# Block-causal attention and a gated FFN in one kernel: softmax's division moved behind P times V, its reciprocals transposed onto the feature partitions, sums kept per group, lag to the transposes 10 -> 6

## The chip, the cores and the metric

The kernel runs on one core of a Trainium2 chip. Its metric is the device time of one execution in microseconds (us); lower is better. Three runs of the kernel before the change took 1388.63, 1390.05 and 1391.88 us, so the median is 1390.05 us.

A core has TensorE (PE in the profile, with its weight loads in a row of their own, PEld), VectorE (DVE), ScalarE (ACT), GpSimd (POOL) and SyncE (SP), which here only issues DMAs. Each engine takes its instructions in the order in which they were built. Matrix products land in PSUM, which has eight banks here, each of 512 fp32 columns on 128 partitions.

## The reference, cut to what matters

```python
batch, n_heads, seq, head_dim = (8, 8, 576, 64)
scores = matmul(q, k.transpose(0, 1, 3, 2)) / sqrt(64)
scores = where(pos[:, None] // 64 >= pos[None, :] // 64, scores, -1e9)
scores = scores - max(scores, axis=-1, keepdims=True)
attn = exp(scores)
attn = attn / (sum(attn, axis=-1, keepdims=True) + 1e-09)
x = matmul(attn, v).transpose(0, 2, 1, 3).reshape(4608, 512)
h = x @ w_in                                    # 512 -> 2048
P = a[0] + a[1] * h + a[2] * h**2 + a[3] * h**3
Q = 1.0 + abs(b[0]) * abs(h) + abs(b[1]) * h**2
out = (P / (Q + 1e-6)) @ w_out                  # 2048 -> 512
```

All inputs and the output are fp32. Every large product is taken as three products of values that are split into a high and a low part.

## The kernel before, in words

**Attention** goes by pairs of heads: 8 batches of 4 pairs make 32 *visits*. A visit has five query tiles t = 0 to 4 (64 queries, then four times 128, lists `NQ` and `Q0`) with 64 to 576 keys (`NK`), and two heads j; each (t, j) is a *step*, so a visit has ten steps and the program 320. The names of tiles carry the visit first: s24_1_0_0 is a score tile of visit 24, query tile 1, head 0.

For a step, `scores` (L403) multiplies queries by keys into a PSUM bank (L421, L422, and L425 for the mask), and VectorE takes the negated row maximum (L426). One step later `expo` (L432) has ScalarE write exp into p and add each row's sum into sm (L438). After the second head of a tile, GpSimd adds 1e-9 to the sums (L445), VectorE takes the reciprocals (L446), and GpSimd multiplies them into p: the first 64 keys of both heads go into pk (L447), the other keys stay in place (L451). `transp` (L455) transposes pk and p by TensorE through PSUM (L470; for t = 0 the source has 64 partitions), ScalarE copies out the high part (L475) and VectorE the low part (L476), into pt0, pt1 and pt2. `pv` (L479) multiplies V by them (L489), for group g = 0 (t = 0, 1, 2, 320 queries) and g = 1 (t = 3, 4, 256 queries). The result has the features of both heads on the 128 partitions and queries along the row. ScalarE and VectorE split it into the tile x (L492, L493; tag "xs", one buffer), and a DMA on SyncE's queue stores it in the scratch tensor xscr (L494).

`prep` (L344) makes the next visit's transposed q and k (tp, L355) and the tiles kq by DMA. `vprep` (L374) splits V (L382, L383).

**The FFN** takes 18 chunks of 256 tokens in two phases, 10 of the 16 hidden blocks in phase 0 and 6 in phase 1. A *unit* is a chunk and two hidden blocks: `first` (L190) is 24 products into h (L201) and the first elementwise work, `recip` (L216) and `split` (L228) the rest of it, `second` (L238) 12 products (L250). A chunk can be loaded (L185) when the batches that hold its tokens are in xscr. Phase 0 is woven into the attention; what is left of it and phase 1 run after it.

**The order.** `attn_steps` (L502) emits scores at step k, `expo` at k + 1, and for j = 1 `transp` at k + min(ALAG3, nxt[k] - 1); nxt is the distance to the same tile of the next visit, 10, so ALAG3 = 10 gives a lag of 9. `pv` comes one step behind the transposes of t = 2 and t = 4. The loop at L565 emits FFN units by step: from E0 = 40 + ALAG3 + 3 on (53), up to the chunks that are ready. The Tile layer then orders each engine's instructions with a timeline of its own, so an instruction may stand elsewhere in its engine's queue than it was emitted, and a tile waits until its buffer's last reader is done. Scores, transposes, products and FFN share PSUM: five banks in ps_a, one in ps_h, two in ps_o.

## Time and profile before

| what | value |
|---|---|
| median of three runs | 1390.05 us |
| the profiled execution, its own time | 1389.48 us |
| its span, first to last instruction | 1387.7 us |
| PE busy in the span | 1294.4 us (93%) |
| PE weight loads busy | 1165.6 us (84%) |
| DVE, ACT, POOL busy | 1029.0, 909.7, 955.3 us (74, 66, 69%) |
| first FFN product (L201) | about 134 us |
| last store of an attention result (L494) issued | 982.1 us |

So the span has three stretches: attention and the splitting of the weights alone (0 to 134 us), attention woven with FFN phase 0 (134 to 985 us), and the FFN alone (985 us to the end). In a row of a view by groups stand line, engine, operation, tile written and tiles read, shape, count, then busy us in total, mean ns of one, and idle time of the engine ahead of it with what ended it. In a row of the stretches stand the engines' busy time in that stretch, the instructions in brackets, the granted TensorE clock, the share of the DMA engines and GB/s. A busy PE is not PE at its peak, since products are pipelined: of two that follow each other the second starts before the first ends.

### The profile page before, as it was taken

To read this page: it belongs to the slowest core of one execution; us is meant where nothing else is said; L and a number is where in the kernel's file an instruction comes from. 1 tells how busy PE (TensorE), PEld (TensorE's weight loads), DVE (VectorE), ACT (ScalarE), POOL (GpSimd) and SP (SyncE) were. 2 spreads that over 40 slices of the span, in tenths; PEclk is the share of its full clock that TensorE was granted. 3 is DMA by queue.
4 is the path that set the end of the run, shared out by engine and by line. 5 is a ranking of instruction groups with operands and counts; after the bars stand their busy time and mean duration, and the time that the engine had idled before them with its cause. 6 is when DMAs were issued, how large, how long until landed. Compare 5 with 4: busy or idle time off the path is not lost.

```text
span 1387.7 us, 25820 instructions
## 1 busy us (share of the span) xinstructions
PE 1294.4 (93%) x8736; PEld 1165.6 (84%) x8736; DVE 1029.0 (74%) x2048; ACT 909.7 (66%) x2250; POOL 955.3 (69%) x1240
## 2 busy tenths in 40 slices
PE   4677899999899989999999999999989999999998
PEld 3567788989788878888989999999979998999897
DVE  5898877788778867887767777766756676776665
ACT  4676777777677766776767777776545555555553
POOL 4888877687777757777767676766556655565564
PEclk9787899999999999999999999999999999999999
DMA  9778566666656665675654565651711333333332
GB/s 214 199 196 234 146 148 161 158 165 184 149 142 154 162 167 141 156 178 136 164 133 113 150 151 123 152 139 46 259 59 60 107 122 122 122 122 122 122 122 91
DMA packets 225635, 200.93 MB, mean 145 GB/s; under 512 B 132064, under 2 KB 195552, under 8 KB 225504
## 3 DMA queue, kind: packets, MB, share of 16 engines
q1 hardware_dynamic: 225440, 199.28, 54.2%
q8 instruction: 70, 1.15, 0.3%
q14 instruction: 61, 0.50, 0.1%
q0 software_dynamic: 64, 0.00, 0.0%
HBM read 98.57 MB, written 44.04 MB: 103 GB/s over the span
## 4 chain that ended last, share of the span: by engine, by line
PE 72%; DVE 9%; DMA 6%; POOL 5%; ACT 4%; issue 2%; SPq 1%; DVEq 0%; POOLq 0%; ACTq 0%
PE h L201 26%; PE o L250 25%; PE o L489 9%; PE t L470 4%; PE s L421 3%; PE s L422 3%; PE tp L355 2%; DMA x<-xscr 2%; DMA kq<-hl 2%; DVE nm L426 1%; ACT p L438 1%; POOL gl L234 1%; DVE v L225 1%; DVE u L224 1%; DMA xscr<-x 1%
## 5 line engine op out<-in xcount | busy, mean ns | idle before, releaser
L201 PE MATMUL h<-x,wih 128*128 128x256 f32 x2304 | 446.3, 289 | 12.0 <-DMA x<-xscr 7.9
L201 PEld LDWEIGHTS h<-x,wih 128*128 128x128 f32 x2304 | 372.3, 194 | 21.6 <-issue 7.6
L201 PE MATMUL h<-x,wil 128*128 128x256 f32 x1152 | 331.0, 287 | 0.0
L250 PE MATMUL o<-woh,gl 128*128 128x512 f32 x576 | 232.2, 403 | 7.9 <-POOL gl L234 6.8
L210 POOL TENSOR_SCALAR v<-u,bab 128x512 f32<-128x512 f32 x144 | 120.2, 835 | 165.0 <-ACT u L208 162.6
L250 PE MATMUL o<-woh,gh 128*128 128x512 f32 x576 | 227.9, 396 | 0.0
L250 PE MATMUL o<-wol,gh 128*128 128x512 f32 x576 | 227.0, 394 | 0.0
L426 DVE TENSOR_REDUCE nm<-s 128x1 f32<-128x288 f32 (+4 forms) x384 | 161.4, 427 | 84.8 <-PE s L425 49.9
L201 PEld LDWEIGHTS h<-x,wil 128*128 128x128 f32 x1152 | 223.2, 194 | 0.4
L234 POOL TENSOR_TENSOR gl<-s,gh 128x512 fp32r<-128x512 f32 x144 | 188.4, 1309 | 50.2 <-ACT gh L233 47.2
L438 ACT ACTIVATE p<-s,nm 128x288 f32<-128x288 f32 (+4 forms) x384 | 184.6, 484 | 47.1 <-DVE nm L426 34.8
L211 POOL TENSOR_TENSOR u<-v,u 128x512 f32<-128x512 f32 x144 | 190.2, 1321 | 9.8
L451 POOL TENSOR_SCALAR p<-p,rc 128x128 f32<-128x128 f32 (+3 forms) x256 | 165.0, 656 | 31.6 <-DVE rc L446 29.3
L208 ACT ACTIVATE u<-h 128x512 f32<-128x512 f32 x144 | 86.0, 597 | 123.5 <-PE h L201 116.9
L218 ACT ACTIVATE v<-u,qcb 128x512 f32<-128x512 f32 x144 | 104.6, 726 | 92.0 <-POOL u L211 91.4
L421 PE MATMUL s<-kq 128*128 128x256 f32 (+3 forms) x384 | 136.3, 357 | 24.0 <-DMA kq<-hl 11.2
L212 DVE TENSOR_TENSOR s<-s,h 128x512 f32<-128x512 f32 x144 | 98.6, 685 | 69.8 <-ACT s L209 68.9
L250 PEld LDWEIGHTS o<-woh,gl 128*128 128x128 f32 x576 | 109.4, 190 | 28.3 <-POOL gl L234 9.0
L250 PEld LDWEIGHTS o<-wol,gh 128*128 128x128 f32 x576 | 108.7, 189 | 22.4
L250 PEld LDWEIGHTS o<-woh,gh 128*128 128x128 f32 x576 | 109.3, 190 | 16.0
L470 PE MATMUL t<-ident,p 128*128 128x128 f32 (+1 forms) x672 | 113.0, 279 | 7.2 <-POOL p L451 2.3
L422 PE MATMUL s<-kq 128*128 128x256 f32 (+3 forms) x384 | 119.0, 312 | 0.0
(105 smaller groups left out, 2993.6 us busy)
## 6 DMA issues: line engine op xcount, KB each, us to landing
kq<-hl SPq DMA_DIRECT2D x64, 432.0 KB, 4.2
x<-xscr SPq DMA_DIRECT2D x96, 256.0 KB, 3.6
kq<-hl SPq DMA_DIRECT2D x64, 288.0 KB, 5.4
xscr<-x SPq DMA_DIRECT2D x32, 320.0 KB, 4.7
qr<-in_q_dram SPq DMA_DIRECT2D x64, 144.0 KB, 2.8
kr<-in_k_dram SPq DMA_DIRECT2D x64, 144.0 KB, 2.7
kq<-hl SPq DMA_DIRECT2D x64, 144.0 KB, 4.9
pscr<-os SPq DMA_DIRECT2D x18, 512.0 KB, 3.3
```

The lines of the kernel that those rows point to most:

```text
L201: nc.tensor.matmul(h[:, j, :], lhsT=w[:, dc, fs], rhs=xs[dc // 2][:, dc % 2, hl, :], start=(dc == 0 and i == 0), stop=(dc == 3 and i == 2))
L210: nc.gpsimd.tensor_scalar(out=vt, in0=ut, scalar1=b1, scalar2=b0, op0=ALU.mult, op1=ALU.add)
L211: nc.gpsimd.tensor_tensor(out=ut, in0=vt, in1=ut, op=ALU.mult)
L234: nc.gpsimd.tensor_tensor(out=gl.rearrange("p j t -> p (j t)"), in0=st, in1=gh.rearrange("p j t -> p (j t)").bitcast(F32), op=ALU.subtract)
L250: nc.tensor.matmul(self.o[m], lhsT=g[:, j, ms], rhs=w[:, f, :], start=(u == 0 and j == 0 and i == 0), stop=(u == nu - 1 and j == 1 and i = ...
L421: nc.tensor.matmul(ps[:, :ww], lhsT=kq[:, 0, qs], rhs=kq[:, 1, c0:c0 + ww], start=True, stop=False)
L422: nc.tensor.matmul(ps[:, :ww], lhsT=kq[:, 0, qs], rhs=kq[:, 2, c0:c0 + ww], start=False, stop=not last)
L426: nc.vector.reduce_max(out=nm[:nq, j, i:i + 1], in_=ps[:nq, :w], axis=AX.X, negate=True)
L438: nc.scalar.activation(out=pt[:nq, j, c0:c0 + w], in_=banks[i][:nq, :w], func=AF.Exp, bias=nm[:nq, j, 0:1], scale=1.0, accum_out=sm[:nq, j ...
L451: nc.gpsimd.tensor_scalar(out=pt[:nq, jj, 64:n], in0=pt[:nq, jj, 64:n], scalar1=rc[:nq, jj:jj + 1], scalar2=1.0, op0=ALU.mult, op1=ALU.mult)
L470: nc.tensor.transpose(ps[:, i, :nq], src, ident[:nq, :nq])
L489: nc.tensor.matmul(o[:, s0:w], lhsT=vblock(vv, x), rhs=pp, start=(x == 0 and i == 0), stop=(x == nb - 1 and i == 2))
```

## The change

`expo` no longer divides. The row sums go straight into two tiles that stay for the whole program, sums[0] for t = 0, 1, 2 and sums[1] for t = 3, 4 (with a third column for the second piece of t = 4). GpSimd only copies the first 64 keys into pk (now L447, a copy, and none for t = 0). After t = 2 and after t = 4 one addition of 1e-9 (L455) and one reciprocal (L456) serve the whole group. The tile of t = 0 becomes p0 with 128 partitions whose lower half stays zero, and all transposes take 128 partitions (L474).

A new function `scale` stands right behind the transposes of t = 2 and t = 4: for each query tile of the group GpSimd spreads the reciprocals of both heads over 2 x 64 columns (rb, L491, one buffer), TensorE transposes that into a bank r (L492), and ScalarE copies the bank into the second half of the tile x (L495). In `pv` VectorE multiplies the product by it (L511), ScalarE takes the high part (L512), and GpSimd, no longer VectorE, takes the low part (L513). The store to xscr therefore waits for GpSimd. ALAG3 goes from 10 to 6: the transposes stand 6 steps behind instead of 9, E0 becomes 49, and the other bounds that hold ALAG3 move with it.

```diff
--- before.py
+++ after.py
@@ -31,7 +31,7 @@
 KQB = 3
 XB = 3
 HOLD = 6
-ALAG3 = 10
+ALAG3 = 6
 OFFS = {5:(0,3,5)}
 G1 = 0
 W0 = 36
@@ -305,6 +305,11 @@
         pt1 = [apers.tile([128, 4, 256], F32R, name=f"pt1{x}") for x in "hl"]
         pt2 = [apers.tile([128, 9, 256], F32R, name=f"pt2{x}") for x in "hl"]
 
+        p0 = apers.tile([128, 2, 64], F32, name="p0")
+        nc.vector.memset(p0[64:128], 0.0)
+        sums = [apers.tile([128, 3, 2], F32, name=f"sum{g}") for g in range(2)]
+        nc.vector.memset(sums[0], 1.0)
+
         vpad = [apers.tile([128, 128 + 4 * 192], F32R, name=f"vp{x}") for x in "hl"]
         for x in pt1:
             nc.vector.memset(x[:, 2:4, 0:128].bitcast(F32), 0.0)
@@ -404,13 +409,12 @@
             s = st_[p]
             nq = NQ[t]
             if j == 0:
-                pt = att.tile([128, 2, NK[t]], F32, name=f"p{p}_{t}", tag=f"p{t}", bufs=1)
+                pt = att.tile([128, 2, NK[t]], F32, name=f"p{p}_{t}", tag=f"p{t}", bufs=1) if t > 0 else p0
+                nm = att.tile([128, 2, 2], F32, name=f"nm{p}_{t}", tag="nm", bufs=4)
 
                 pk = att.tile([128, 2, 64], F32, name=f"pk{p}_{t}", tag="pk", bufs=2) if t > 0 else pt
-                nm = att.tile([128, 2, 2], F32, name=f"nm{p}_{t}", tag="nm", bufs=4)
-                sm = att.tile([128, 2, 2], F32, name=f"sm{p}_{t}", tag="sm", bufs=4)
-                s[t] = (pt, pk, nm, sm)
-            pt, pk, nm, sm = s[t]
+                s[t] = (pt, pk, nm)
+            pt, pk, nm = s[t]
             kq = s["kq", j]
             qs = slice(Q0[t], Q0[t] + 128)
             banks = []
@@ -432,28 +436,28 @@
         def expo(p, t, j):
             s = st_[p]
             nq, n = NQ[t], NK[t]
-            pt, pk, nm, sm = s[t]
+            pt, pk, nm = s[t]
+            g, i0 = ((0, t), (1, t - 3))[t > 2]
             banks = s.pop((t, j))
             for i, (c0, w) in enumerate(pieces(t)):
                 nc.scalar.activation(out=pt[:nq, j, c0:c0 + w], in_=banks[i][:nq, :w], func=AF.Exp,
-                                     bias=nm[:nq, j, 0:1], scale=1.0, accum_out=sm[:nq, j, i:i + 1])
-            if j == 0:
+                                     bias=nm[:nq, j, 0:1], scale=1.0,
+                                     accum_out=sums[g][:nq, i0 + i, j:j + 1])
+            if j == 1 and t > 0:
+                nc.gpsimd.tensor_copy(out=pk, in_=pt[:, :, 0:64])
+            if j == 0 or t not in (2, 4):
                 return
-            rc = att.tile([128, 2], F32, name=f"rc{p}_{t}", tag="rc", bufs=4)
-            if t == 4:
-                nc.gpsimd.tensor_tensor(out=sm[:, :, 0], in0=sm[:, :, 0], in1=sm[:, :, 1], op=ALU.add)
-            nc.gpsimd.tensor_scalar_add(rc[:nq], sm[:nq, :, 0], 1e-9)
-            nc.vector.reciprocal(rc[:nq], rc[:nq])
-            nc.gpsimd.tensor_tensor(out=pk[:nq], in0=pt[:nq, :, 0:64],
-                                    in1=rc[:nq].unsqueeze(2).to_broadcast([nq, 2, 64]), op=ALU.mult)
-            if t > 0:
-                for jj in range(2):
-                    nc.gpsimd.tensor_scalar(out=pt[:nq, jj, 64:n], in0=pt[:nq, jj, 64:n],
-                                            scalar1=rc[:nq, jj:jj + 1], scalar2=1.0,
-                                            op0=ALU.mult, op1=ALU.mult)
+
+            nt = (3, 2)[g]
+            rc = att.tile([128, 3, 2], F32, name=f"rc{p}_{g}", tag="rc", bufs=2)
+            if g:
+                nc.gpsimd.tensor_tensor(out=sums[1][:, 1], in0=sums[1][:, 1], in1=sums[1][:, 2], op=ALU.add)
+            nc.gpsimd.tensor_scalar_add(rc[:, :nt], sums[g][:, :nt], 1e-9)
+            nc.vector.reciprocal(rc[:, :nt], rc[:, :nt])
+            s["rc", g] = rc
 
         def transp(p, t):
-            pt, pk, _, _ = st_[p].pop(t)
+            pt, pk, _ = st_[p].pop(t)
             nq = NQ[t]
             nb = 1 + 2 * t
             groups = {1: [1], 3: [1, 2], 5: [1, 4], 7: [4, 3], 9: [3, 3, 3]}[nb]
@@ -463,11 +467,11 @@
                 for i in range(gn):
                     x = blk + i
                     if x == 0:
-                        src = pk[:nq].rearrange("q j k -> q (j k)")
+                        src = pk.rearrange("q j k -> q (j k)")
                     else:
                         key = 64 + 128 * ((x - 1) // 2)
-                        src = pt[:nq, (x - 1) % 2, key:key + 128]
-                    nc.tensor.transpose(ps[:, i, :nq], src, ident[:nq, :nq])
+                        src = pt[:, (x - 1) % 2, key:key + 128]
+                    nc.tensor.transpose(ps[:, i, :], src, ident)
                 (hi, lo), b0, c0 = ((pt2, blk, Q0[t] - 320) if t > 2 else (pt0, 0, Q0[t]) if blk == 0 else
                                     (pt1, blk - 1, Q0[t] - 64))
                 dh = hi[:, b0:b0 + gn, c0:c0 + nq]
@@ -475,6 +479,20 @@
                 nc.scalar.copy(out=dh, in_=ps[:, :gn, :nq])
                 nc.vector.tensor_tensor(out=dl, in0=ps[:, :gn, :nq], in1=dh.bitcast(F32), op=ALU.subtract)
                 blk += gn
+
+        def scale(p, g):
+
+            rc = st_[p].pop(("rc", g))
+            w = (320, 256)[g]
+            ps = bank(p, f"r{p}_{g}")
+            c0 = 0
+            for i, n in enumerate(((64, 128, 128), (128, 128))[g]):
+                rb = att.tile([128, 2, D], F32, name=f"rb{p}_{g}_{i}", tag="rb", bufs=1)
+                nc.gpsimd.tensor_copy(out=rb, in_=rc[:, i].unsqueeze(2).to_broadcast([128, 2, D]))
+                nc.tensor.transpose(ps[:, c0:c0 + 128], rb.rearrange("q j d -> q (j d)"), ident)
+                c0 += n
+            xs = st_[p]["xs", g] = att.tile([128, 2, 320], F32R, name=f"x{p}_{g}", tag="xs", bufs=1)
+            nc.scalar.copy(out=xs[:, 1, :w].bitcast(F32), in_=ps[:, :w])
 
         def pv(p, g):
             b, hp = divmod(visits[p][0], NPAIR)
@@ -488,9 +506,11 @@
                 for i, (vv, pp) in enumerate(((vh, lo), (vh, hi), (vl, hi))):
                     nc.tensor.matmul(o[:, s0:w], lhsT=vblock(vv, x), rhs=pp,
                                      start=(x == 0 and i == 0), stop=(x == nb - 1 and i == 2))
-            xs = att.tile([128, 2, 320], F32R, name=f"x{p}_{g}", tag="xs", bufs=1)
-            nc.scalar.copy(out=xs[:, 0, :w], in_=o[:, :w])
-            nc.vector.tensor_tensor(out=xs[:, 1, :w], in0=o[:, :w], in1=xs[:, 0, :w].bitcast(F32), op=ALU.subtract)
+            xs = st_[p].pop(("xs", g))
+            xn = xs[:, 1, :w].bitcast(F32)
+            nc.vector.tensor_tensor(out=xn, in0=o[:, :w], in1=xn, op=ALU.mult)
+            nc.scalar.copy(out=xs[:, 0, :w], in_=xn)
+            nc.gpsimd.tensor_tensor(out=xs[:, 1, :w], in0=xn, in1=xs[:, 0, :w].bitcast(F32), op=ALU.subtract)
             nc.sync.dma_start(out=xscr[b][:, hp, :, g * 320:g * 320 + w], in_=xs[:, :, :w].bitcast(F32))
 
         items = [(i, t, j) for i, (_, ts) in enumerate(visits) for t in ts for j in range(2)]
@@ -526,6 +546,7 @@
                         lag = min(ALAG3, nxt[k] - 1)
                         at(k + lag, transp, p, t)
                         if t in (2, 4):
+                            at(k + lag, scale, p, t // 4)
                             at(k + lag + 1, pv, p, t // 4)
                             if t == ts[-1] and p + 1 < NV:
                                 at(k + lag + 1, vprep, p + 1)
```

How the order moves. On TensorE at the start of visit 24, the first visit of batch 6, these rows stood before; h0_10_0 is an FFN unit of chunk 10, o0_9 the output of chunk 9, t23 transposes of visit 23, tp25 the preparation of visit 25:

```order
L201 MATMUL h0_10_0_10485<-x0_10_1_10331,wil0_143 128x256
L421 MATMUL s24_0_1_0_9853<-kq24_1_9613 128x256
L422 MATMUL s24_0_1_0_9853<-kq24_1_9613 128x256
L470 MATMUL t23_1_0_9895<-ident_99,pk23_1_9460 128x128
L470 MATMUL t23_1_1_9899<-ident_99,p23_1_9459 128x128 x2
L421 MATMUL s24_1_0_0_9913<-kq24_0_9609 128x256
L422 MATMUL s24_1_0_0_9913<-kq24_0_9609 128x256
L425 LDWEIGHTS mrow_104
L425 MATMUL s24_1_0_0_9913<-mcol_105,mrow_104 128x64
L355 MATMUL tp25_0_0_9919<-ident_99,qr25_9834 128x96 x3
L250 MATMUL o0_9_0_10286<-woh0_144,gl0_9_4_10663 128x512
```

And these stand there now; r23_0 is the bank of the transposed reciprocals, o23_0 the product P times V of visit 23, group 0:

```order
L250 MATMUL o0_10_1_10863<-wol0_150,gh0_10_4_11260 128x512
L425 MATMUL s24_0_0_0_9822<-kq24_0_9618 128x256
L426 MATMUL s24_0_0_0_9822<-kq24_0_9618 128x256
L474 MATMUL t23_2_0_9826<-ident_99,pk23_2_9535 128x128
L474 MATMUL t23_2_1_9830<-ident_99,p23_2_9533 128x128 x4
L492 MATMUL r23_0_9837<-ident_99,rb23_0_0_9838 128x128
L425 MATMUL s24_0_1_0_9850<-kq24_1_9622 128x256
L426 MATMUL s24_0_1_0_9850<-kq24_1_9622 128x256
L507 MATMUL o23_0_9892<-pt0l_129,vph_139 128x320
L507 MATMUL o23_0_9892<-pt0h_128,vph_139 128x320
L507 MATMUL o23_0_9892<-pt0h_128,vpl_140 128x320
L425 MATMUL s24_1_0_0_9916<-kq24_0_9618 128x256
```

Chunk 10 is finished ahead of visit 24 (its last unit is the first row), and chunk 11 comes only near the end of the visit; between two score tiles stand transposes and products of the attention alone, r's among them. Counted over the whole visit, from its first score tile to the next visit's, the order held 77 products of L201 and 24 of L250 and holds 15 and none. In visits 12, 16 and 28 it holds 15 and 12, 24 and 12, and 15 and none, where 70 and 24, 48 and 24, and 70 and 36 stood; in visits 9, 22 and 23 it holds more than it did. From the first score tile of the last visit on, the order holds 1704 and 876 where it held 1752 and 894.

On GpSimd, around the tiles of visit 16, before; gl is FFN work:

```order
L447 TENSOR_TENSOR p16_0_6246<-p16_0_6246,rc16_0_6287 64x128
L451 TENSOR_SCALAR p16_1_6291<-p16_1_6291,rc16_1_6375 128x128 x2
L234 TENSOR_TENSOR gl0_5_4_7421<-s0_5_4_7186,gh0_5_4_7420 128x512
L447 TENSOR_TENSOR pk16_1_6292<-p16_1_6291,rc16_1_6375 128x128
L445 TENSOR_SCALAR rc16_2_6467<-sm16_2_6384 128x2
L451 TENSOR_SCALAR p16_2_6381<-p16_2_6381,rc16_2_6467 128x256 x2
L447 TENSOR_TENSOR pk16_2_6382<-p16_2_6381,rc16_2_6467 128x128
L445 TENSOR_SCALAR rc16_3_6545<-sm16_3_6476 128x2
L451 TENSOR_SCALAR p16_3_6473<-p16_3_6473,rc16_3_6545 128x384 x2
```

And now; rb is the spread reciprocals, x15_1 the low part of visit 15's result, vpl the low part of V, v and u are FFN work:

```order
L491 COPY rb16_0_0_6726<-rc16_0_6525 128x128
L388 TENSOR_TENSOR vpl_140<-vr16_5795,vph_139 128x4x64 x2
L513 TENSOR_TENSOR x15_1_6455<-x15_1_6455 128x256
L447 COPY pk16_3_6530<-p16_3_6528 128x128
L210 TENSOR_SCALAR v0_6_0_7177<-u0_6_0_7176,bab_115 128x512
L211 TENSOR_TENSOR u0_6_0_7176<-v0_6_0_7177,u0_6_0_7176 128x512
L447 COPY pk16_4_6605<-p16_4_6603 128x128
L454 TENSOR_TENSOR sum1_137<-sum1_137 128x2
L455 TENSOR_SCALAR rc16_1_6694<-sum1_137 128x4
L491 COPY rb16_0_1_6729<-rc16_0_6525 128x128
```

The scalings of p are gone from GpSimd's queue; copies of 128 x 128 and the low part of x stand in it, and the second rb of a group stands behind FFN work.

## The prediction

> **What bounds the kernel now.** I read the page's busy times first, then three stretches, then what TensorE (PE) waits for in each, then single transposes in the order of time, and last single visits.
>
> ```profile
> span 1387.7 us, 25820 instructions
> PE 1294.4 (93%) x8736; PEld 1165.6 (84%) x8736; DVE 1029.0 (74%) x2048; ACT 909.7 (66%) x2250; POOL 955.3 (69%) x1240
> ```
>
> ```profile
> 0.00:134.00 134.00, 86.03 (x487) 71.46 (x488) 105.86 (x255) 85.35 (x252) 101.99 (x144) 0.84 0.84 209
> 134.00:985.00 851.00, 817.54 (x5798) 740.72 (x5798) 649.71 (x1413) 606.85 (x1647) 615.82 (x890) 0.99 0.58 147
> 985.00:1387.70 402.70, 390.81 (x2455) 353.40 (x2453) 273.47 (x381) 217.48 (x352) 237.50 (x207) 0.99 0.37 119
> ```
>
> The stretches decide how the change is to be priced. In the first, attention and weights alone, PE is busy for 86 of 134 us, while VectorE and GpSimd are at 106 and 102 us; work saved on them may help there. In the second, attention with FFN phase 0 (visits 5 to 31, 27 of them), PE is busy for 817.5 of 851 us: what PE gains or loses counts nearly in full, and GpSimd (616 us) has room. The third holds no attention and is not touched.
>
> What ends PE's idle time, in the second stretch and then in the first (total us, times, longest):
>
> ```profile
> PE h L201 <- DMA x<-xscr: 6.7, 3, 2.6
> PE o L489 <- DVE pt0l L476: 6.0, 4, 2.0
> PE o L250 <- POOL gl L234: 4.7, 6, 1.4
> ```
>
> ```profile
> PE t L470 <- POOL p L451: 2.9, 5, 0.9
> ...
> PE t L470 <- POOL pk L447: 0.8, 1, 0.8
> ```
>
> PE hardly waits for the scaled p that the change does away with: 3.7 us in all, and only where FFN work is not there to cover it.
>
> **a. The transposes of the reciprocals: +14.7 us.** `scale` adds 5 per visit, 160 in all. What one costs is the distance to the next start, not its duration. A run of them, then a single one between FFN products:
>
> ```profile
> 803.03 1.04 PE L470 MATMUL t<-ident,p 128*128 128x128 f32 x8
> ```
>
> ```profile
> 700.39 0.28 PE L201 MATMUL h<-x,wih 128*128 128x256 f32 x1
> 700.52 0.27 PE L470 MATMUL t<-ident,pk 128*128 128x128 f32 x1
> 700.54 0.36 PE L201 MATMUL h<-x,wih 128*128 128x256 f32 x1
> 700.74 0.28 PE L201 MATMUL h<-x,wil 128*128 128x256 f32 x1
> 700.86 0.40 PE L201 MATMUL h<-x,wih 128*128 128x256 f32 x2
> ```
>
> Eight take 1.04 us, of which the last one's own 0.27 overlaps what follows: (1.04 - 0.27) / 7 = 0.11. Singly: two FFN products in a row are 0.40 - 0.28 = 0.12 apart; from 700.39 to 700.74 there are two of them and the transpose, 0.35 - 0.24 = 0.11. In the first stretch PE has idle time for them; in visits 5 to 31 they cost 135 x 0.109 = 14.7 us. The Trainium skill, page "TensorE: Matmul & The Clock Gate", Part 4, puts a 128 x 128 transpose at about 275 ns in a kernel and says that transposes do not count as busy for the clock gate; by its figure the term would be an estimated 37 us. The trace agrees with the 275 as a duration (0.27 above), not as a distance, and with some 25 transposes a visit the granted clock of the second stretch is 0.99.
>
> **b. The transposes of t = 0: -7.6 us.** They go from 64 partitions to 128, and this is the one gain on PE. Around a 64-partition one:
>
> ```profile
> 660.73 0.28 PE L201 MATMUL h<-x,wil 128*128 128x256 f32 x1
> 660.94 0.27 PE L470 MATMUL t<-ident,p 64*128 64x64 f32 x1
> 661.14 0.50 PE L201 MATMUL h<-x,wih 128*128 128x256 f32 x2
> 661.48 0.28 PE L201 MATMUL h<-x,wil 128*128 128x256 f32 x1
> ```
>
> From 660.73 to 661.48 there are three FFN products, 0.36, and this transpose: 0.75 - 0.36 = 0.39. [...] A 128-partition one costs 0.11, so 0.28 each is saved, 27 x 0.28 = 7.6.
>
> **c. Visits without FFN cover: +2.3 us.** The order moves FFN products ahead of visits 12, 16, 24 and 28, the first of batches 3, 4, 6 and 7, and leaves these nearly bare. Work done earlier is no loss; an idle PE is. Cut at the first score product of a visit, the first row below is visit 24, the next three are visits 1 to 3, which have no FFN, the last two are visits 12 and 16 as they ran before:
>
> ```profile
> 723.00:752.00 29.00, 27.59 (x210) 25.38 (x208) 22.54 (x50) 22.79 (x61) 21.84 (x31) 1.00 0.54 131
> ```
>
> ```profile
> 35.00:60.00 25.00, 17.82 (x106) 15.21 (x104) 20.94 (x49) 14.77 (x43) 21.70 (x28) 0.77 0.74 192
> 60.00:88.00 28.00, 20.26 (x114) 16.79 (x114) 24.58 (x59) 20.15 (x63) 23.90 (x33) 0.82 0.74 196
> 88.00:109.00 21.00, 15.58 (x99) 13.30 (x100) 19.45 (x48) 17.20 (x56) 19.68 (x28) 0.84 0.84 212
> ```
>
> ```profile
> 351.00:384.00 33.00, 28.46 (x207) 25.76 (x207) 23.22 (x50) 20.52 (x60) 24.17 (x33) 1.00 0.58 147
> 478.00:511.00 33.00, 27.04 (x183) 24.22 (x182) 20.15 (x46) 18.79 (x55) 19.02 (x31) 0.95 0.64 170
> ```
>
> ```profile
> 800.33 0.39 PE L250 MATMUL o<-wol,gh 128*128 128x512 f32 x1
> 800.56 0.39 PE L250 MATMUL o<-woh,gl 128*128 128x512 f32 x1
> ```
>
> An L250 takes 0.23. Visit 24 held 77 x 0.12 + 24 x 0.23 = 14.7 us of FFN in 29 us, so attention's own PE work is 14.3; now it has 14.3 + 15 x 0.12 + 5 x 0.11 - 0.28 = 16.4. How long does a bare visit last? At least ScalarE's work, 17.4 us by the mean of the three bare ones; at most their mean length, 24.7. Those had VectorE at 65 of 74 us with weight splitting, which is over by then, so I take 19.6: PE idles for 3.2 us, 12.8 in four (ends 1.0 and 8.3 each, so 4 and 33). They replace what visits 12 and 16 idled already, 4.5 + 6.0 = 10.5 by the last two rows of the visits. 12.8 - 10.5 = 2.3, with ends -6 and 23.
>
> **d. The end of the attention: +2 us.** From the last visit on the order holds 48 L201 and 18 L250 fewer, 9.9 us of cover. PE idled next to nothing there (27.59 of 29 in visit 24 is the kind), so the loss lies between 0 and 9.9.
>
> **e. The start: -2 us.** The 3.7 us of waits above can go, and VectorE has three reciprocals of 0.16 us fewer per visit, 2.4 us in five. VectorE still splits weights at 88%, and each FFN chunk is stored later by a longer chain. Ends -6 and 0.
>
> **f. GpSimd: -2 us.** Costs by the groups:
>
> ```profile
> L447 POOL TENSOR_TENSOR pk<-p,rc 128x128 f32<-128x128 f32 x128 | 62.8, 491 | 46.3 <-PE t L470 41.8 <-DVE rc L446 2.8
> L383 POOL TENSOR_TENSOR vpl<-vr,vph 128x256 fp32r<-128x256 f32 x64 | 52.1, 830 | 22.0 <-PE o L489 16.6 <-ACT vph L382 3.9 <-DMA kq<-hl 0.6
> L445 POOL TENSOR_SCALAR rc<-sm 128x2 f32<-128x2 f32 x128 | 35.9, 280 | 42.1 <-ACT p L438 33.9
> ...
> L446 DVE RECIPROCAL rc<-rc 128x2 f32<-128x2 f32 x128 | 20.5, 160 | 28.9 <-POOL rc L445 25.9
> ```
>
> ```profile
> L451 POOL TENSOR_SCALAR p<-p,rc 128x128 f32<-128x128 f32 (+3 forms) x256 | 165.0, 656 | 31.6 <-DVE rc L446 29.3
> ```
>
> Gone: 165.0 of L451, about 79 of L447 (160 x 0.49), 27 of L445 (96 x 0.28). Added: 288 copies of 128 x 128, which no row shows; between 0.28 (two elements) and 0.49 (same shape, two inputs) I take 0.40, 115 us; and 64 low parts of x at 0.83 to 1.0, some 58. Net -98 us, 3 us a visit, off the path: PE waits 4.7 us for gl, and those mostly end with ScalarE's gh. New are the waits for rb: with one buffer a group's second copy waits for PE's first transpose, and PE's second for the copy. A tenth of a us at 81 of them is 8 us, none is likelier, as other products stand between. So -2, ends -5 and +8. ScalarE's added copies (64) and VectorE's multiplication in place of a subtraction lie beside PE's work at 606.85 and 649.71 of 851 us. The store now waits for GpSimd and stands ahead of the loads of kq on SyncE; no kq wait of PE is in the second stretch, and kq has three buffers: nothing, and about 1.4 us per visit if that cover went.
>
> **The sum.** 14.7 - 7.6 + 2.3 + 2 - 2 - 2 = +7.4 on the profiled execution's 1389.48 (span 1387.7 and 1.8 around it), which lies 0.6 below the median of the three runs: 1396.9, or 1397 with part of that 0.6. Own range 1392 to 1402.
>
> **Rivals.**
>
> 1. *The bare visits crawl.* They last 24.7 us, as visits 1 to 3 did. For it: the chain score, maximum, exp, transposes, copies is the same, and banks are handed over with little work between. Against it: no weights are split. Half to all of c's upper end, 1407 to 1418, say 1410.
> 2. *Faster: the waits at the batch boundaries and the start were GpSimd's doing.* With 98 us off GpSimd and three steps less lag, chunks arrive earlier; c at its low end (-6), e at -4, f at -3: 14.7 - 7.6 - 6 - 4 - 3 = -6, 1384. It decides once these together beat the 7.1 of a and b. For it: GpSimd is busy for 102 of the first 134 us. Against it: PE's named waits for it are 3.7 and 4.7 us.
> 3. *The one buffer of x.*
>
> ```profile
> L494 SPq DMA_DIRECT2D xscr<-x x64: 359/389/2017, 46.8 to 982.1; - x64
> ...
> DMA to landing us min/median/max: 2.1/2.8/7.4
> ```
>
> ```profile
> L492 ACT CAST x<-o 128x320 fp32r<-128x320 f32 x32 | 13.6, 426 | 11.0 <-PE o L489 8.2 <-PE s L425 1.3 <-issue 1.2
> ```
>
> ScalarE now writes x before the product is there. Copy, multiplication and cast at 0.43 each, low part 0.9, issue 0.39 and landing 2.8 hold it for 5.4 us at least, twice a visit, and ScalarE stands still if the next copy comes too soon. In the new order the two groups of a bare visit stand about 3 us of PE work apart: 2.5 us each, 10 in four, 1407.
> 4. *Hidden.* The added transposes fall into the 33 us that PE idles in the second stretch, and b to f cancel: 1390.
> 5. *A transpose costs its duration.* 135 x 0.27 = 36 in place of 14.7: 1418. The rows of a speak against it, and the skill's page above is the rule for it.
>
> **How the numbers follow.** The forecast has 0.35, rival 1 0.17, rival 2 0.23, rival 3 0.10, rival 4 0.12, rival 5 0.03. The range 1384 to 1412 leaves out about half of rival 2, and parts of 1 and 5. A measurement tells about 0.2% from no change (2.8 us: 1387.3 to 1392.8). Faster is rival 2, 0.23; the same is rival 4 and the forecast's low edge, 0.16; the rest, 0.61, is slower.
>
> **What would show it.** In the profile after: 160 transposes of L492 some 0.11 from the next start (a); t = 0's transposes without the gaps (b); PE idle in visits 12, 16, 24 and 28 and dense elsewhere (c); GpSimd about 98 us less busy (f). If PE's idle time in the second stretch shrinks by more than 7 us, or bare visits run at PE's pace, the forecast is too high; if ScalarE waits for the store of x, or PE for r's copies, too low.

## The result and the profile after

| | median us | range, executions |
|---|---|---|
| after | 1450.38 | 1444.07 to 1453.17, 4 |
| before, beside it | 1390.97 | 1388.63 to 1399.25, 4 |

The change makes the kernel slower: ratio 1.041, 95% interval 1.038 to 1.0441. The forecast of 1397 had the sign right and fell short by 53 us; the range (1384 to 1412) missed too. The profiled execution of after took 1444.07 us, 54.6 more than that of before. Medians here and below leave out one execution in the slow state, of a_last13 (1819.47 us at a granted clock of 0.65).

The page of after, span and busy times:

```profile
span 1442.0 us, 26058 instructions
PE 1316.2 (91%) x8896; PEld 1180.2 (82%) x8896; DVE 1028.8 (71%) x1954; ACT 934.0 (65%) x2314; POOL 854.8 (59%) x1080
```

GpSimd is 100.5 us less busy, as forecast (98), and TensorE (PE) 21.8 us more. The rest of the 54 us is PE standing idle. Both kernels cut at the first score product of visit 5 and of visit 31, before and then after (us, then PE, PEld, DVE, ACT, POOL busy, granted clock, DMA share, GB/s):

```profile
0.00:139.00 139.00, 91.03 (x524) 76.39 (x524) 109.74 (x262) 89.11 (x264) 106.63 (x149) 0.84 0.85 211
139.00:935.00 796.00, 763.05 (x5404) 690.06 (x5403) 614.19 (x1339) 571.99 (x1556) 583.06 (x843) 0.98 0.60 151
935.00:1387.70 452.70, 440.29 (x2813) 399.14 (x2811) 305.10 (x447) 248.58 (x432) 265.63 (x249) 0.99 0.36 114
```

```profile
0.00:143.00 143.00, 91.98 (x551) 77.83 (x552) 102.26 (x236) 89.04 (x265) 78.04 (x118) 0.84 0.80 193
143.00:998.00 855.00, 793.44 (x5595) 712.69 (x5594) 624.52 (x1286) 600.96 (x1628) 519.06 (x722) 0.98 0.57 143
998.00:1442.00 444.00, 430.74 (x2755) 389.70 (x2753) 302.06 (x435) 243.99 (x423) 257.70 (x242) 0.99 0.36 116
```

Visits 5 to 30 take 59 us longer, and PE idles 61.6 of them instead of 33.0. Some 10 of the 59 are FFN work that has moved forward: the last stretch is 8.7 us shorter. What ended PE's waits in this stretch of after (total us, times, longest):

```profile
PE s L425 <- DMA kq<-hl: 10.2, 7, 2.9
PE h L201 <- DMA x<-xscr: 8.8, 6, 3.1
PE t L474 <- ACT p L443: 8.4, 6, 3.3
PE s L425 <- ACT p L443: 6.5, 7, 1.7
PE tp L360 <- DVE pt2l L480: 2.8, 3, 1.5
PE r L492 <- POOL rb L491: 2.7, 6, 0.7
```

No single wait carries it. The spread copies rb, whose wait is the new one on PE, end only 2.7 us of its idle time. The same copies look quite different from GpSimd's side. Its groups, then what ended its waits:

```profile
L491 POOL COPY rb<-rc 128x128 f32<-128x128 f32 x160 | 58.4, 365 | 129.7 <-PE r L492 117.5 <-DVE rc L456 9.3 <-PE s L429 1.1
```

```profile
POOL v L210 <- ACT u L208: 175.5, 99, 5.5
POOL rb L491 <- PE r L492: 117.5, 81, 3.5
```

GpSimd stands still 81 times, 117.5 us in all, ahead of a copy, because rb has one buffer and the copy before it has not been transposed yet. One such place, GpSimd first, then PE's two transposes r:

```profile
682.34 0.22 POOL L455 TENSOR_SCALAR rc<-sum 128x4 f32<-128x4 f32 x1
684.85 0.29 POOL L491 COPY rb<-rc 128x128 f32<-128x128 f32 x1 [2.28 <-PE r L492]
687.84 0.29 POOL L491 COPY rb<-rc 128x128 f32<-128x128 f32 x1 [2.70 <-PE r L492]
688.89 1.28 POOL L234 TENSOR_TENSOR gl<-s,gh 128x512 fp32r<-128x512 f32 x1 [0.76 <-ACT gh L233]
```

```profile
684.51 0.27 PE L492 MATMUL r<-ident,rb 128*128 128x128 f32 x1
...
687.50 0.27 PE L492 MATMUL r<-ident,rb 128*128 128x128 f32 x1
```

For 5 us GpSimd does two copies of 0.29 us. PE does not wait here: it works through other products and reaches each r late. What is late is everything queued on GpSimd behind the copies. By which path that reaches PE is not traced further.

Second, SyncE's queue. Before, kq's DMAs stand ahead of v's loads; after, v's stand ahead of kq's. The first piece is before, visit 8's end, the second after, visit 16's end:

```profile
254.96 0.46 SPq L369 DMA_DIRECT2D kq<-hl  x1
255.47 0.60 SPq L370 DMA_DIRECT2D kq<-hl  x1
256.11 1.68 SPq L371 DMA_DIRECT2D kq<-hl  x1
...
262.73 0.49 SPq L339 DMA_DIRECT2D vr<-in_v_dram  x1
```

```profile
529.91 1.38 SPq L344 DMA_DIRECT2D vr<-in_v_dram  x1
531.34 0.59 SPq L345 DMA_DIRECT2D vr<-in_v_dram  x1
531.97 0.52 SPq L344 DMA_DIRECT2D vr<-in_v_dram  x1
532.53 0.59 SPq L345 DMA_DIRECT2D vr<-in_v_dram  x1
533.22 0.48 SPq L374 DMA_DIRECT2D kq<-hl  x1
```

With the transposes three steps earlier, `vprep` frees the tile of v three steps earlier too, so these loads no longer come after kq. At 540.86 PE waits 2.8 us for this kq.

Third, the bare visits 12, 16, 24 and 28 of after:

```profile
383.00:406.00 23.00, 19.91 (x149) 17.25 (x147) 13.10 (x33) 16.16 (x50) 8.84 (x21) 1.00 0.74 206
509.00:534.00 25.00, 20.29 (x155) 17.79 (x154) 16.55 (x42) 17.44 (x53) 14.55 (x24) 1.00 0.83 229
786.00:808.00 22.00, 17.76 (x136) 15.17 (x135) 12.72 (x32) 14.75 (x47) 8.74 (x20) 1.00 0.63 157
907.00:931.00 24.00, 18.32 (x133) 16.11 (x132) 12.81 (x34) 14.80 (x50) 8.67 (x20) 0.93 0.61 154
```

They last 23.5 us on the mean, near rival 1's 24.7 and above the forecast's 19.6; PE idles 94 - 76.3 = 17.7 us in them by busy time.

Fourth, the granted clock. It was 0.961 to 0.968 in the four executions of after (mean 0.963) and 0.967 to 0.975 in those of before beside the experiments (mean 0.971). In the traces it falls to one half for 3.4 us or a multiple of that. In before, after, a_rbp and b_tr5 each fall comes right behind 3.4 us in which PE idled for at least 1.2. In these rows stand the length, the five engines' busy time, the granted clock, the DMA share and GB/s. One such place in after:

```profile
478.00:481.40 3.40, 1.06 (x10) 0.82 (x8) 0.00 (x0) 0.15 (x1) 2.30 (x2) 1.00 0.25 90
481.40:488.20 6.80, 5.83 (x18) 4.87 (x19) 5.27 (x9) 4.49 (x12) 1.16 (x2) 0.50 0.13 46
```

So here a wait of PE costs more than its own length. In visits 5 to 30 the clock is halved for 24 us in before and 41 in after, an estimated 12 and 20.5 us lost.

### The profile page after: what moved, and what is told of

It is laid out like the page before. It is cut to its first block, busy times and chain, and to the rows that moved or that the text cites. A ratio compares the mean times of both kernels' runs of the same rounds, so it can differ in the third digit from the quotient of the medians.

```text
span 1442.0 us, 26058 instructions
## 1 busy us (share of the span) xinstructions
PE 1316.2 (91%) x8896; PEld 1180.2 (82%) x8896; DVE 1028.8 (71%) x1954; ACT 934.0 (65%) x2314; POOL 854.8 (59%) x1080
## 4 chain that ended last, share of the span: by engine, by line
PE 68%; DMA 10%; DVE 7%; POOL 5%; ACT 4%; SPq 3%; issue 2%; POOLq 0%; DVEq 0%; ACTq 0%
PE h L201 25%; PE o L250 23%; PE o L507 9%; DMA kq<-hl 4%; PE t L474 4%; PE s L425 3%; DMA x<-xscr 3%; PE s L426 2%; PE tp L360 2%; DMA kr<-in_k_dram 2%; DVE nm L430 1%; POOL u L211 1%; POOL vpl L388 1%; POOL gl L234 1%; ACT p L443 1%
## 5 line engine op out<-in xcount | busy, mean ns | idle before, releaser
L201 PE MATMUL h<-x,wih 128*128 128x256 f32 x2304 | 440.4, 288 | 15.5 <-DMA x<-xscr 8.9
L201 PEld LDWEIGHTS h<-x,wih 128*128 128x128 f32 x2304 | 368.2, 192 | 26.3 <-DMA x<-xscr 9.9
L201 PE MATMUL h<-x,wil 128*128 128x256 f32 x1152 | 330.6, 287 | 0.0
L250 PE MATMUL o<-woh,gl 128*128 128x512 f32 x576 | 234.4, 407 | 4.4 <-POOL gl L234 4.2
L250 PE MATMUL o<-woh,gh 128*128 128x512 f32 x576 | 230.0, 399 | 0.0
L250 PE MATMUL o<-wol,gh 128*128 128x512 f32 x576 | 228.8, 398 | 0.0
L201 PEld LDWEIGHTS h<-x,wil 128*128 128x128 f32 x1152 | 221.7, 192 | 0.1
L425 PE MATMUL s<-kq 128*128 128x256 f32 (+3 forms) x384 | 138.7, 362 | 47.9 <-DMA kq<-hl 29.4
L491 POOL COPY rb<-rc 128x128 f32<-128x128 f32 x160 | 58.4, 365 | 129.7 <-PE r L492 117.5
L250 PEld LDWEIGHTS o<-woh,gl 128*128 128x128 f32 x576 | 110.5, 192 | 23.5 <-POOL gl L234 5.9
L250 PEld LDWEIGHTS o<-wol,gh 128*128 128x128 f32 x576 | 109.8, 191 | 22.6
L425 PEld LDWEIGHTS s<-kq 128*128 128x128 f32 x384 | 77.2, 201 | 59.3 <-issue 23.8
L250 PEld LDWEIGHTS o<-woh,gh 128*128 128x128 f32 x576 | 110.4, 192 | 16.5
L474 PE MATMUL t<-ident,p 128*128 128x128 f32 x672 | 113.0, 282 | 10.8 <-ACT p L443 3.3
```

What stands on the lines that cost most here:

```text
L201: nc.tensor.matmul(h[:, j, :], lhsT=w[:, dc, fs], rhs=xs[dc // 2][:, dc % 2, hl, :], start=(dc == 0 and i == 0), stop=(dc == 3 and i == 2))
L250: nc.tensor.matmul(self.o[m], lhsT=g[:, j, ms], rhs=w[:, f, :], start=(u == 0 and j == 0 and i == 0), stop=(u == nu - 1 and j == 1 and i = ...
L425: nc.tensor.matmul(ps[:, :ww], lhsT=kq[:, 0, qs], rhs=kq[:, 1, c0:c0 + ww], start=True, stop=False)
L474: nc.tensor.transpose(ps[:, i, :], src, ident)
```

## The experiments

Eighteen kernels were run. The medians, the ratios to the kernel before on the same chip and their 95% intervals:

| run | what it is | us | ratio, interval |
|---|---|---|---|
| b_lag6 | before, lag 6 | 1431.95 | 1.0293, 1.0262 to 1.0323 |
| a_lag10 | after, lag 10 | 1432.05 | 1.0296, 1.0265 to 1.0327 |
| a_noscale | after without the scaling | 1401.63 | 1.0082, 1.0053 to 1.0111 |
| a_const | after, r from the identity | 1411.19 | 1.0148, 1.0116 to 1.0179 |
| a_rbx | after, two copies in x's tile | 1443.96 | 1.0381, 1.0353 to 1.0408 |
| a_rbx10 | the same, lag 10 | 1413.66 | 1.0157, 1.0133 to 1.018 |
| b_lag6_offs | b_lag6, q and k prepared earlier | 1426.65 | 1.0249, 1.0219 to 1.0279 |
| b_p0 | before, t = 0 on 128 partitions | 1391.24 | 0.9992, 0.9972 to 1.0012 |
| a_constrb | a_const with unread copies | 1417.24 | 1.0175, 1.0143 to 1.0208 |
| a_vr8 | after, v loaded later | 1440.93 | 1.0341, 1.0299 to 1.0383 |
| a_last13 | after, FFN starts as before | 1440.97 | 1.0348, 1.0318 to 1.0378 |
| a_lowdve | after, low part on VectorE | 1463.58 | 1.0512, 1.0481 to 1.0542 |
| a_rbp | after, free buffers for rb | 1412.11 | 1.0134, 1.0105 to 1.0162 |
| a_rbp_vr8 | the same, v loaded later | 1399.88 | 1.0059, 1.0039 to 1.0079 |
| b_tr5 | before, five more transposes | 1398.91 | 1.0046, 1.0028 to 1.0063 |
| a_noscale10 | a_noscale, lag 10 | 1391.18 | 0.9989, 0.9973 to 1.0005 |
| c_lag7 | a_rbp_vr8, lag 7 | 1427.19 | 1.025, 1.0219 to 1.0281 |
| c_offs024 | a_rbp_vr8, q and k prepared earlier | 1411.74 | 1.0139, 1.0116 to 1.0163 |

The first theories: A, the spread copies of the reciprocals through their one buffer; B, the shorter lag; C, the longer end of a visit with the store behind it.

**Which half of the change.** The lag alone, the lag undone, the scaling left out, and the scaling without GpSimd's copies:

```diff
-ALAG3 = 10
+ALAG3 = 6
```

That is b_lag6, on the kernel before; a_lag10 is the reverse, on the kernel after.

> The kernel before, with the lag to the transposes at 6 steps and nothing else. Theory A (the spread copies of the reciprocals, through one buffer, draw out the transposes of a group, hold a PSUM bank and push FFN work ahead of the batches' first visits): 1391 us, within 4. Theory B (the shorter lag does the damage): 1430 or more. Theory C (the longer end of a visit: multiplication, high part, low part on GpSimd, and the store behind them on SyncE's queue): 1391, within 4.

> The changed kernel with the lag back at 10 (9 steps). Theory A: 1440 or more, since all of the scaling is still there. Theory B: about 1400, the kernel before plus the 7 us of the transposes. Theory C: 1440 or more.

```diff
-                rb = att.tile([128, 2, D], F32, name=f"rb{p}_{g}_{i}", tag="rb", bufs=1)
-                nc.gpsimd.tensor_copy(out=rb, in_=rc[:, i].unsqueeze(2).to_broadcast([128, 2, D]))
-                nc.tensor.transpose(ps[:, c0:c0 + 128], rb.rearrange("q j d -> q (j d)"), ident)
+                nc.tensor.transpose(ps[:, c0:c0 + 128], ident, ident)
```

That is a_const; a_noscale also drops the transposes, the bank and ScalarE's copy, and has VectorE copy the product.

> The changed kernel without the transposes of the reciprocals, their copies on GpSimd, their PSUM bank and ScalarE's copy out of it; VectorE copies the product where it multiplied. The division is left out. Theory A: about 1383, the kernel before less the 7.6 us that t = 0's transposes save. Theories B and C: 1425 to 1435, the changed kernel less 15 us of transposes and what their own waits cost.

> The changed kernel with the five transposes of a visit taken from the identity tile, not from copies that GpSimd spreads; bank, ScalarE's copy and everything behind them stay. The product is multiplied by the identity's columns, not by reciprocals. Theory A: 1395 to 1402, the kernel before plus the 7 us of TensorE's added work. Theory B or C: 1440 or more. If the cost lies in the fifth PSUM user alone, the bank of r, it stays above 1430 too.

Measured: 1432, 1432, 1402 and 1411. No theory holds alone, and a_lag10, a_noscale and a_const lie outside the ranges of all three. B foretold b_lag6 and fails at a_const; A comes nearest at a_const, 9 us above its range, and fails at b_lag6; C fails at a_const, which keeps the longer end of a visit. Of the 59 us, 39 hang on the copies (1450.4 - 1411.2); lag and scaling do not add up, since each alone costs 41 and both together 59.

**The copies: load, place or buffer.** In a_constrb the copies are made and nobody reads them. In a_rbx the second and third copy go to the half of x that is still free:

```diff
-                nc.tensor.transpose(ps[:, c0:c0 + 128], rb.rearrange("q j d -> q (j d)"), ident)
+                nc.tensor.transpose(ps[:, c0:c0 + 128], ident, ident)
```

```diff
-                rb = att.tile([128, 2, D], F32, name=f"rb{p}_{g}_{i}", tag="rb", bufs=1)
+                rb = (att.tile([128, 2, D], F32, name=f"rb{p}_{g}", tag="rb", bufs=1) if i == 0 else
+                      xs[:, 0, 128 * i - 128:128 * i].bitcast(F32).rearrange("q (j d) -> q j d", j=2))
```

The second is a_rbx, with the tile x allocated ahead of the loop; a_rbx10 adds ALAG3 = 10.

> The changed kernel with the transposes of r taken from the identity tile, as in the run that came to 1411, but with GpSimd's 160 spread copies still made into rb, where nobody reads them. The product is multiplied by the identity's columns, not by reciprocals. Theory D1 (what costs time is that TensorE waits for copies that stand in GpSimd's queue behind other work): 1408 to 1416, as without the copies. Theory D2 (GpSimd's 56 us of copies delay GpSimd's other work, and that costs the time): 1435 to 1450.

> The changed kernel, in which only the first spread copy of a group goes to rb; the second and third go to the half of the tile x that is free until the product is there. So no copy waits for the transpose of the one before, and all work stays. Theory A (the one buffer): 1411 to 1416, as with the identity in place of the copies, since GpSimd's 56 us of copies lie off the path. If it was the copies themselves on GpSimd, not their buffer: 1435 to 1450. If the tile x, now taken earlier, becomes the new wait: 1425 to 1440.

> The same with the lag back at 10. If the buffer and the lag each cost what they did alone, this is the kernel before plus the 7 us of TensorE's work plus what the longer end of a visit costs: 1398 to 1402. If the lag only cost time together with GpSimd's scaling of p, as in the kernel before with lag 6: 1411 to 1416, the same as with lag 6. If something of the scaling is still open, 1420 or more.

Measured: 1417, 1444, 1414. The load is worth about 6 us (1417.2 - 1411.2, each with an interval of some 4 us to either side), so D2 falls. a_rbx seemed to refute the buffer, until its profile is read from GpSimd's side. What ended GpSimd's waits in a_rbx:

```profile
POOL x L493 <- DMA xscr<-x: 95.3, 37, 6.1
```

The wait for PE had become a wait for the store of x, nearly as long. The test had moved the stall and not removed it. One run does not fit so simply. In a_rbx10 GpSimd waits nearly as long, 77.8 us for the store and 22.2 for PE:

```profile
POOL x L493 <- DMA xscr<-x: 77.8, 42, 5.5
```

Yet it takes 30 us less than a_rbx, and 18 less than a_lag10, where GpSimd waits 108.9 us for r. So the length of the stall does not set its price alone; with the longer lag it costs less, and why is open. A buffer that is really free was needed. With a lag of 6 the tile of p for t = 1 is free when group 0 is scaled, and that of t = 3 for group 1:

```diff
+            tg = (1, 3)[g]
+            rbs = att.tile([128, 2, NK[tg]], F32, name=f"rb{p}_{g}", tag=f"p{tg}", bufs=1).rearrange("q j k -> q (j k)")
             for i, n in enumerate(((64, 128, 128), (128, 128))[g]):
-                rb = att.tile([128, 2, D], F32, name=f"rb{p}_{g}_{i}", tag="rb", bufs=1)
+                rb = rbs[:, 128 * i:128 * i + 128].rearrange("q (j d) -> q j d", j=2)
```

> The changed kernel, complete and with lag 6, in which the spread copies of a group lie side by side in a tile that is free at that time: those of t = 0, 1, 2 in the buffer of p for t = 1, those of t = 3, 4 in the buffer of p for t = 3. So GpSimd waits neither for TensorE's transposes of r nor for the store of x before a copy. Theory G (GpSimd stands still at its second and third copy, 118 us in all with one buffer and 95 with the halves of x, and everything behind these copies comes late): 1412 to 1420, as with copies that nobody reads. If the place of the copies in the chain costs the time, with or without a buffer: 1435 to 1450.

Measured: 1412.11, at the lower edge of theory G. Same work, same lag, 38 us less (its profiled execution, 1406.41, lies 6 below the median, as that of after does). GpSimd's copies in a_rbp, and PE in its visits 5 to 30:

```profile
L493 POOL COPY rb<-rc 128x128 f32<-128x128 f32 x160 | 49.7, 345 | 33.2 <-PE t L474 27.8 <-DVE rc L456 2.7 <-DVE u L224 2.2
```

```profile
143.00:960.00 817.00, 776.08 (x5569) 700.70 (x5568) 615.59 (x1281) 593.49 (x1623) 505.46 (x720) 0.98 0.59 150
```

The idle time ahead of the copies falls from 129.7 to 33.2 us and PE's idle time in the stretch from 61.6 to 40.9. The other 17 of the stretch's 38 us stand in PE's busy time (793.44 to 776.08); the clock is halved there for 27 us instead of 41, at most an estimated 7 of the 17.

A rival is the order, which the Tile layer makes anew: counted from a visit's first score product to the next visit's, visits 12, 16, 24 and 28 hold 15, 24, 15 and 15 products of L201 in after, and 48, 24, 59 and 77 in a_rbp. But a_rbx fills them too, with 54, 48, 83 and 62, and is nearly as slow as after. L201 in its visit 24:

```profile
771.80:805.50 33.70, 11.57 (x83) 10.55 (x83) 1.00 0.54 131
```

So fuller visits alone do not give the 38 us, and the buffer is shown as their cause: freeing it is the only edit. How much of the 38 comes by the wait itself, and how much by the order that goes with it, no run separates. The Trainium skill, page "Trainium Kernel Development and Optimization", section "Best Practices", asks for double buffers to overlap DMA with compute; here the missing buffer lay between two engines, and no run tests it for a DMA.

**SyncE's queue.**

```diff
                             at(k + o0, load, p + 1)
+                            at(k + 8, loadv, p + 1)
```

This is a_vr8; `loadv` holds the loads of v, taken out of `load`. a_rbp_vr8 is the same on a_rbp.

> The changed kernel with the loads of the next visit's v emitted 8 steps into a visit in place of 0. With a lag of 6 the tile of v comes free earlier, and its four loads stand ahead of or between those of kq on SyncE's queue; now they stand behind. Theory E (SyncE's queue makes kq late): TensorE's waits for kq, some 30 us in all before and after the first FFN product, mostly go, 1420 to 1430. If those waits only stand in for others: 1440 to 1450.

> The same, and v's loads emitted 8 steps into a visit. If the two costs lie apart: 7 to 10 us below the run with the free buffers alone. If kq's lateness is covered once GpSimd runs freely: within 4 us of it.

Measured: 1440.9 (9.5 us less than after, whose interval meets its own) and 1399.9 (12.2 less than a_rbp, clear of noise and above the 7 to 10 expected). So this cost lies apart from the buffer's. Theory E is half right at most, since a_vr8 lies in the range of the other theory, that these waits stand in for others. PE's wait for kq over the whole program goes from 30.1 to 25.1 us, a_rbp first, then a_rbp_vr8:

```profile
PE s L425 <- DMA kq<-hl: 30.1, 12, 5.1
```

```profile
PE s L429 <- DMA kq<-hl: 25.1, 10, 4.5
```

That explains 5 of the 12; the rest is not traced. Of the 13 us between the two profiled executions, 7 lie ahead of visit 5, whose first score product comes at 136 instead of 143 us.

**The lag without the scaling.**

> The changed kernel without the transposes of the reciprocals, their copies, bank and ScalarE's copy (1402 with lag 6), and with the lag back at 10. The division is left out. If the lag of 6 costs time by itself, through the order (k's preparation and kq later, v's loads ahead of them): 1385 to 1394. If the lag costs time only where GpSimd's work stands between exp and the transposes: 1399 to 1404, as with lag 6.

The edit is ALAG3 = 10 on a_noscale. Measured: 1391.18, that is 10.5 us less than with lag 6. So the lag costs some 10 us with no scaling at all. That is about the size of what v's loads cost (12); that it is the same cost is not shown, since they were not moved in this kernel.

**The lag in the kernel before** costs far more, 41 us. On b_lag6:

```diff
-OFFS = {5:(0,3,5)}
+OFFS = {5:(0,2,3)}
```

> The kernel before with the lag at 6, and with the next visit's q transposes one step earlier and its k transposes two steps earlier, so that there is as much TensorE work between k's transposes and the visit's first score product as before (17.4 us of products in the order, against 11.9 with the lag alone and 15.7 before). Theory B1 (the lag costs time because it moves the old visit's transposes and products ahead of the preparation of k, so that kq comes late): 1391 to 1405, and TensorE's waits for kq, 24.6 us with the lag alone, gone. Theory B2 (the lag costs time because the transposes wait for p, scaled on GpSimd): 1425 to 1432, as with the lag alone.

Measured: 1426.65; B1 falls. PE's waits, b_lag6 first, then b_lag6_offs:

```profile
PE s L421 <- DMA kq<-hl: 45.5, 19, 4.7
```

```profile
PE s L421 <- DMA kq<-hl: 27.9, 12, 5.3
PE t L470 <- POOL p L451: 12.0, 9, 3.2
PE o L250 <- POOL gl L234: 11.3, 11, 5.8
```

With kq earlier, GpSimd's scaled p and FFN's gl are late instead. This speaks for B2, GpSimd's scaling as the limit at the shorter lag, but no run takes that scaling away by itself, so it is argued and not shown.

**TensorE's own terms.**

```diff
+                for i in range(gn, gn + {(2, 0): 3, (4, 0): 1, (4, 1): 1}.get((t, gi), 0)):
+                    nc.tensor.transpose(ps[:, i, :], ident, ident)
```

```diff
-                    nc.tensor.transpose(ps[:, i, :nq], src, ident[:nq, :nq])
+                    nc.tensor.transpose(ps[:, i, :], src, ident)
```

The first is b_tr5, into columns that t's banks leave free; the second b_p0, with p0 and its zeroed lower half as in after.

> The kernel before with five transposes of the identity added to each visit, in columns of PSUM banks that its own transposes leave free; nobody reads them. Term a of the prediction by the distance of starts: 160 times 0.109, 17 us, 13 to 20 as visits without FFN may hide some: 1404 to 1411. By a transpose's duration, 0.27 each: 1434. If TensorE's idle time hides them: 1391 to 1395.

> The kernel before with t = 0's transposes on 128 partitions and nothing else. Term b of the prediction: 1391 less 32 times 0.28 us, 1382 to 1384. If TensorE's gaps at those transposes were filled anyway, 1389 to 1393. If the order that results is worse, above 1393.

Measured against before beside them: +6.9 by the medians (interval 3.9 to 8.8) where the distances give 17.4, and -1.1 by the ratio (-3.9 to 1.7) where they give -9.0. For b_tr5 the stretches of its one profile (span 1397.0 us, 9.3 above that of before) tell where the difference went, cut like those of before above:

```profile
0.00:135.00 135.00, 89.51 (x547) 75.63 (x547) 107.00 (x257) 90.04 (x261) 103.25 (x145) 0.87 0.83 213
135.00:949.00 814.00, 780.60 (x5537) 705.69 (x5537) 617.99 (x1345) 574.31 (x1558) 586.49 (x847) 0.98 0.59 148
949.00:1397.00 448.00, 438.31 (x2816) 397.05 (x2814) 309.39 (x447) 248.61 (x431) 264.22 (x250) 1.00 0.36 115
```

In visits 5 to 30 the 130 added transposes cost 18 us, all that the distances give (14.2) and an estimated 5 of halved clock; PE idles 33 us there in both kernels, so nothing was hidden. Before's first and last stretch are 4 and 5 us longer than these, at a lower granted clock (0.84 and 0.99 against 0.87 and 1.00). Over the whole, b_tr5's ten executions had a mean of 0.976 beside 0.971, an estimated 8 us. So the total is small by a gain elsewhere, where these transposes do not bind; what brought that gain is open.

In b_p0 a t = 0 transpose between FFN products:

```profile
564.25 0.29 PE L201 MATMUL h<-x,wil 128*128 128x256 f32 x1
564.38 0.27 PE L473 MATMUL t<-ident,p 128*128 128x128 f32 x1
564.40 0.48 PE L201 MATMUL h<-x,wih 128*128 128x256 f32 x2
564.72 0.28 PE L201 MATMUL h<-x,wil 128*128 128x256 f32 x1
```

From 564.25 to 564.72 there are three products (0.36) and the transpose, 0.11, where before it was 0.39. The place is 0.28 us faster and the kernel is not: over the span PE is 4.1 us less busy and idles 6.8 more.

**Misses that close a door.** The FFN's start as before, and the low part of x on VectorE:

```diff
-        LAST = ALAG3 + 3
+        LAST = 13
```

```diff
-            nc.gpsimd.tensor_tensor(out=xs[:, 1, :w], in0=xn, in1=xs[:, 0, :w].bitcast(F32), op=ALU.subtract)
+            nc.vector.tensor_tensor(out=xs[:, 1, :w], in0=xn, in1=xs[:, 0, :w].bitcast(F32), op=ALU.subtract)
```

> The changed kernel with the start of the FFN and the steps at which its chunks count as ready put back to where they stood before the change (53 in place of 49), lag 6 otherwise. Fewer visits are nearly bare of FFN: 16, 12 and 28 stay thin, 24 is full. Theory F (the loss is FFN work that runs ahead and leaves visits bare): 1425 to 1438. If the bare visits are a symptom and not the cause: 1440 to 1455.

> The changed kernel with the low part of x back on VectorE, so that the store waits for VectorE, as before the change, and GpSimd is 58 us less busy. Theory C (the longer end of a visit on GpSimd, with the store behind it): 1430 or less. If the end of the visit is not the cause: 1443 to 1455.

a_last13 came to 1441, 9 us less than after. It fills visit 24 alone (72 products of L201; 24 each in visits 12, 16 and 28), so it bounds the bare visits' part less well than a_rbx does. a_lowdve came to 1464, 13 us more: the end of the visit on GpSimd is not the cost. In it GpSimd waits longer for PE's r than in after:

```profile
L491 POOL COPY rb<-rc 128x128 f32<-128x128 f32 x160 | 59.7, 373 | 159.6 <-PE r L492 145.5 <-DVE rc L456 12.5 <-PE t L474 0.3
```

**A version that beats both?** From a_rbp_vr8:

> The version with free buffers for the spread copies and v's loads at step 8 (1400), with a lag of 7 in place of 6, the longest at which those buffers are free. If the rest of the lag's cost is k's late preparation: 1390 to 1396, as the order then holds 15.5 us of products between k's transposes and the visit's first score product (11.7 with lag 6, 15.7 in the kernel before). If the rest is TensorE's added work alone: 1396 to 1402.

> The same version with lag 6, and the next visit's q and k transposed one step earlier each (steps 2 and 4 in place of 3 and 5); 16.1 us of products stand between k's transposes and the first score product. If the rest of the lag's cost is k's late preparation: 1390 to 1396; if it is TensorE's added work alone: 1396 to 1402.

Edits: ALAG3 = 7, and OFFS (0,2,4). Measured: 1427 and 1412, against 1400. Both expectations fail, and no version found beats the kernel before. Each edit makes the Tile layer order all engines anew. In c_lag7 PE waits for the last batches' x in the third stretch, 12.0 us in two waits, a_rbp_vr8 not at all:

```profile
PE h L201 <- DMA x<-xscr: 12.0, 2, 9.8
```

What else is in these 12 and 27 us is open. So a difference of some 10 us between two of these kernels is credited to an edit here only where a profile row moves with it.

## Why the prediction was right or wrong

- **The sum**, as measured: 38.3 for rb's one buffer (after to a_rbp), 12.2 for v's loads (to a_rbp_vr8), and 7.8 from there to the kernel before. That the last comes near a less b (14.7 - 7.6) is no test of them: it also holds the rest of the change, and each total moves with the clock.
- **f failed, and with it the forecast.** It named the right place, "with one buffer a group's second copy waits for PE's first transpose", and priced it on PE, a tenth of a us at 81 places, "none is likelier, as other products stand between". PE's direct wait is indeed small (2.7 us in the stretch). But the products that stand between are what GpSimd waits for: 1.45 us on the mean of 81 waits (117.5 / 81; the prediction's 81 were other places, three in each of 27 visits), with FFN work and pk behind. The price was 38 us, not -2 with an end at +8. That is the mis-sized term.
- **f's sentence on SyncE** looked at the wrong neighbour. The store was taken as kq's new obstacle; it was v's loads, which the lag lets forward. Priced at nothing, or 1.4 us a visit if the cover went; measured 12.
- **a** held, as far as b_tr5 shows it: 130 transposes cost 18 us in 26 of the 27 visits for which 14.7 was forecast, though the kernel as a whole took only 6.9 more. Rival 4 (hidden) falls, as PE's idle time in that stretch stays at 33 us, and so does rival 5, by which 160 would cost 43: the row below, of after, has 288 ns for one, a duration and not a price. The Trainium skill's 275 ns, page "TensorE: Matmul & The Clock Gate", Part 4, measured there with bf16, agrees with that duration.

```profile
L492 PE MATMUL r<-ident,rb 128*128 128x128 f32 x160 | 46.1, 288 | 9.3 <-DVE pt0l L480 4.7 <-POOL rb L491 4.0 <-issue 0.4
```

- **b** was right in place (0.39 to 0.11) and worth about nothing in sum: "what PE gains or loses counts nearly in full" held for a's loss in its stretch, and not for b's gain in the whole, which went into PE's idle time.
- **c** was right about the visits and too low about their length (23.5 us, rival 1). Putting the FFN's start back gives 9 us, and a_rbx, with these visits filled, is no faster, so they are a symptom more than the cause.
- **Rival 3** (x's one buffer) had a right kind of mechanism at the wrong buffer: ScalarE waits 9.1 us for x's store in all of after. **Rival 2** falls: GpSimd was relieved by 100 us and the time lost there was a wait, not work. **d** and **e** were not isolated; the start came out 4 us longer (139 to 143) where e forecast -2.

## What to carry over

When a copy on one engine feeds another through a single buffer, price the wait on the engine that refills the buffer, not only on the one that reads it: here the producer stood still for as long as the reader's queue had other work ahead of the read, and all that was queued behind it on the producer came late. Look for a tile that is free at that moment before adding one, and check on the profile that the new place does not bring another wait. Test a term of TensorE alone, and read the result in the stretch that the term belongs to: +6.9 us in the whole was +18 there.

## What the runs showed of the hardware

A transpose from 64 partitions between products of 128 cost 0.39 us from start to start and one from 128 partitions 0.11, both t = 0's transpose between FFN products. GpSimd's spread copy of 128 x 128 fp32 took 0.29 us undisturbed and 0.365 on the mean; the low part of 320 or 256 columns took 0.862 on the mean. The granted clock fell to one half for 3.4 us or a multiple, in the traces of before, after, a_rbp and b_tr5 each time behind 3.4 us in which PE had idled for 1.2 or more. Among the 11 executions of a_rbp_vr8 the fastest had 1393.08 us at a granted clock of 0.978, the slowest 1405.84 at 0.970.
